# A planned attention and MLP kernel: its order learns when loads land, v's column bounds are taken later, and the first normalization is divided anew

## The chip, the cores and the metric

The kernel runs on one core of one Trainium2 chip. A core has five engines with a queue each, which run side by side and wait for one another through semaphores: TensorE (PE in the profile, its weight loads PEld), VectorE (DVE), ScalarE (ACT), GpSimd (POOL) and SyncE (SP), which here issues every DMA. Matrix products land in PSUM, eight banks of 2 KB in each of 128 partitions; everything else lives in SBUF. The metric is the device time of one execution in microseconds (us), the median over runs; lower is better.

## What is computed

One block: a layer norm modulated by a condition `c`, attention with 32 heads of width 16 over 2048 rows, a gated residual, then a second modulated norm, a mixer that shifts rows by one or two, and an MLP of width 1792. Cut to what matters here:

```python
mod = (silu(c) @ w_mod).reshape(1, 6, 1, -1)
sa, ca, ga, sb, cb, gb = (mod[:, i] for i in range(6))
h = layernorm(x) * (1 + ca) + sa
q, k, v = split_heads(h @ wqkv)                 # 32 heads, 16 wide
p = softmax(q @ k.T * 16 ** -0.5)
x = x + ga * (merge_heads(p @ v) @ wo)
h = layernorm(x) * (1 + cb) + sb
g = shift_rows(gelu(layernorm(h) @ w1))         # by +1, -1, +2, -2 in four quarters
x1 = h + g @ w2
x = x + gb * (x1 + gelu(layernorm(x1) @ w3) @ w4)
```

## The kernel before

**One order, written by a planner.** The program is not left to a scheduler: while it is built, the class `Sched` keeps a clock for each engine (`sch.T`, with "P" for TensorE and "S" for SyncE's DMA queue), a price for each operation, and decides what is issued next. The prices and the constants at the top of the file are only the planner's; the chip runs the order that comes out, each engine its own queue in sequence. So a constant that adds no instruction can move many.

**Ahead of attention.** The 2048 rows of x come in four chunks of 512 (`ci` 0 to 3). `ln1` takes statistics of four tiles of 128 rows on VectorE (L383, L384), their inverse deviation on GpSimd (L387, L388), and applies the norm tile by tile: on ScalarE (L562) for the tiles listed in `LNA[ci]`, else on VectorE (L559). `ln1_T` transposes on TensorE (L626) and modulates: for the columns in `LNV[ci]` ScalarE writes the high part (L635) and VectorE the whole (L638); else ScalarE does both (L631, L652). The low part of the split is taken on GpSimd for the columns in `LNG[ci]`, else on VectorE (both L644). `PST`, `PAP` and `PTR` rank these chains by chunk, lower first. Products of q, k and v in split precision (L372, L374, L376) follow; q, k and v are stored to DRAM.

**The bound of v.** `v_weights(a)` makes, for each half `a` of the heads, a bound of every column of v: TensorE sums (L825), `bound` clips (L831), then `cols` does three things on VectorE in one piece: two reductions against the identity, which bring the bound from a row into a column (`vcol`, L836), and the reciprocal of the row (L838). Then GpSimd scales the weights of v by that reciprocal (L844) and they are split (L471, L473). `vcol` is read when the pieces of the output projection are scaled (L914). The reductions write their unneeded product into one of the six `qk` buffers.

**Attention.** There are 64 units (4 chunks of queries by 16 pairs of heads) of 16 steps; a step is 128 keys, so there are 1024. Maxima run 24 steps (`LEAD`) ahead of scores: a row of work is one matmul for a maximum (mb, L1033) reduced on VectorE (L1029) beside one matmul of scores (sc, L1049) whose exponential ScalarE takes (L1045). When a unit's maxima are done, eight small DMAs write the shift rows into its q tile (qtl<-nm). Of each exponential the high half is used as it is, and the low half is made by GpSimd in one operation (L1104) or by ScalarE in two: `p_low`. Columns are the products with v (pv): high ones (L1130) for each step, low ones (L1127) for each two. Eight buffers (`NPT`) hold exponentials from the scores to the low columns.

**Who goes next.** The main loop turns between rows, columns and fillers. Fillers are everything else: the remaining q, k and v, the splitting of weights, and the whole block behind attention for earlier chunks (`tail`). `cols()` counts the columns that are ready by `col_at`, at most `CMOST`; rows may start when banks are free (`one`) and VectorE is about to run dry (`EARLY`); after rows, columns wait for fillers if the filler credit is over `OFIRST` and enough buffers are free. `DUES` is a curve: by that step so many us of filler should be done, from which the credit per step comes. `do_row` calls `p_low` for steps that lie `PLAG` behind.

**Loads.** `load_unit` brings a unit's q rows (three DMAs), zeros, and k rows (three DMAs); `load_v` brings v for four steps; all on SyncE's queue. `sch.dma` returns a modelled landing time, which these callers drop: the order assumes the data is there. On the chip the semaphores hold TensorE until it is.

Of the kernel before, what the change touches and what calls it, by code (L numbers as in the profile page):

```python
# [21 lines left out]
P = 128  # L22
# [15 lines left out]
DUES = ((20, 67.7), (60, 87.3), (85, 95.9), (122, 115.8), (150, 130.7), (205, 149.7), (245, 167.7),  # L38
        (505, 270.0), (765, 395.7), (1012, 527.8))
BTOP, BLOW = 1200.0, 300.0  # L40
LEAD = 24
LAG = 2
RES0 = 2
DMIN = 600.0
PAP = (1,0,-1,-1)
PST = (1,0,0,1)
PTR = (-1,1,1,0)
TRX = 140.0
DAP = 1000.0
# [35 lines left out]
LNA = ((1,2,3),(0,1,2,3),(3,),(3,))  # L85
LNG = ((0,1),(0,1,2,3),(0,2),(0,2))
LNV = ((),(),(1,2,3),(1,3))
# [12 lines left out]
PTLOW = 3  # L100
BACK = 100.0
EARLY = 200.0
OWE = 1500.0
PX = 265.0
# [239 lines left out]
def kernel(ctx, tc, A_x, A_wqkv, A_wo, B_w1, B_w2, B_w3, B_w4, c, w_mod, out):  # L344
# [272 lines left out]
    def ln1_T():  # L617
        for ci in range(NC):
            x = xt[ci]
            left = [KT]  # L620
            for k in range(KT):
# [31 lines left out]
                sch.chain(*ops, (e, 1320 if e == "G" else 670, low), (None, 0, one), prio=PTR[ci])  # L653
# [106 lines left out]
    direct, near = [], set()  # L760

    def v_tiles(w, a, kts):
        wh, wl = halves(w, KT)
        for kt in kts:
# [19 lines left out]
            def store(kt=kt, w=w):  # L784
                vrs[0] -= 1

                if not a and direct:
                    sch.dma(dma.dma_start, direct[kt // 4][:, kt % 4], w[:, 0])
                    near.add(kt)

                def gone():
                    vlive.remove(kt)
                    done.add(("vk", a, kt))
                    if kt % 4 == 3:
                        done.add(("v", a, kt // 4))
                e = sch.dma(dma.dma_start, Vs[8 * a:8 * a + 8, :, kt, :].rearrange("a p n -> p a n"),
                            w)
                sch.after(e, gone)
# [9 lines left out]
    def v_weights(a):  # L808
# [19 lines left out]
        scr = ab[0][:, :P]  # L828

        def bound():  # L830
            dve.tensor_scalar(vb, b, 1e-30, None, op0=OP.max)  # L831
            sch.free(b)

        def cols():
            for i in range(2):
                dve.tensor_tensor_reduce(out=scr, in0=vb[:, i * P:(i + 1) * P], in1=ident, scale=VHI, scalar=0.0,  # L836
                                         op0=OP.mult, op1=OP.add, accum_out=vcol[:, 2 * a + i:2 * a + i + 1])
            dve.reciprocal(vb, vb)  # L838
            qfree.extend(ts)

        def scaled():
            for i, (f, f3) in enumerate(st):
                c = slice(512 * i, 512 * i + 512)
                sch.chain(("G", 1500, lambda f3=f3: pool.tensor_tensor(f3, f3, vb[:, None, :].to_broadcast([P, 2, 256]),  # L844
                                                                       op=OP.mult)),
                          *split_chain(f, w[:, 0, c], w[:, 1, c], mark(keys[2 + i])), ready=sch.T["D"] + XX)
            done.add(("vcol", a))
        sch.chain(("D", cD(256), bound), ("D", 1900, cols), (None, 0, scaled), bank=b)
# [89 lines left out]
    def load_rows(t, src, pr, cs, to):  # L938
        for i in range(3):
            sch.dma(dma.dma_start, t[i + 1::4, to].bitcast(F32), src[2 * pr * DH:(2 * pr + 2) * DH, i, cs])  # L940
# [48 lines left out]
    def load_unit(u):  # L989
# [7 lines left out]
        load_rows(kst[u % 3], Ks, pr, slice(0, S), slice(0, S))  # L997
# [3 lines left out]
    def load_v(u, i):  # L1001

        if (u, i) in vnext or not u:
# [3 lines left out]
            sch.dma(dma.dma_start, vst[i], Vs[units[u][1], :, 4 * i:4 * i + 4])  # L1007
# [62 lines left out]
    def max_fin(u):  # L1070
# [4 lines left out]
        def shift_rows():  # L1075
            for j in range(2):
                for i in range(2):
                    r = 64 * j + 32 * i
                    for h in range(2):
                        sch.dma(dma.dma_start,  # L1080
# [520 lines left out]
    def before(s):  # L1601
# [12 lines left out]
        if s < VAT[0]:  # L1614
            for kt in range(4):
                if kt not in near and ("vk", 0, kt) in done:
                    near.add(kt)
                    sch.dma(dma.dma_start, vst[0][:, kt % 4], Vs[0, :, kt])
        if s in VAT:
            i = VAT.index(s)  # L1620
            for kt in range(4 * i, 4 * i + 4):
                while kt not in near and ("vk", 0, kt) not in done:
                    sch.step()
                if kt not in near:
                    sch.dma(dma.dma_start, vst[i][:, kt % 4], Vs[0, :, kt])
# [17 lines left out]
    def col_at(y):  # L1643
# [3 lines left out]
        return max(e_hi[s], v_free[0] if s % NKT == 0 else 0.0) if s in e_hi else LATE  # L1647
# [37 lines left out]
    while x < end or pvs or acs:  # L1685
# [14 lines left out]
        if can:  # L1700
# [4 lines left out]
            if one >= LATE:  # L1705
                one = free[need - 1]
            enter = (sch.mode != "r") * (SWITCH + ENTER)
# [87 lines left out]
```

## Time and profile before

| | us |
|---|---|
| median of 3 runs (1980.74 to 1981.08) | 1981.05 |
| the profiled execution | 1979.15 |
| its span, first to last instruction | 1977.4 |

The profile is of one execution. Busy times count an engine as busy while any of its instructions is under way; for TensorE that includes matmuls whose ends are modelled, so a full TensorE is not one at its peak. A window row gives busy time and number of instructions by engine, the granted clock of TensorE (1.00 is full), the busy share of the DMA engines, and GB/s. A row of waits names who waited for whom: us in total, times, longest. "issue" is waiting for nothing that the profile shows. Attention's exponentials run from 91.2 to about 1810 us; before that lies the preparation, after it the tail of the last chunk.

### The profile page before, as it was taken

The page shows a single profiled execution, that of the slowest core. Times are in us where ns is not written, and L with a number is a line of the kernel's source. Part 1 is how long each engine was busy: PE and PEld are TensorE (multiplying, and loading weights), DVE is VectorE, ACT ScalarE, POOL GpSimd, SP SyncE. Part 2 cuts the span into 40 slices and gives each one's busy share as a digit, 9 for nine tenths or more (in the row PEclk, how much of TensorE's full clock was granted, in tenths as well). Part 3 has the DMA queues.
Part 4 walks back from the last instruction along what each step waited for, and adds up shares of the span by engine and source line. Part 5 has one row for each costly group of instructions (what it writes and reads, how often), then busy time and mean ns, then how long its engine had stood idle before and what let it go on. Part 6 is the DMA issues. An engine that isn't in the chain of part 4 may idle for free.

```text
span 1977.4 us, 42253 instructions
## 1 busy us (share of the span) xinstructions
PE 1924.6 (97%) x14472; PEld 1126.1 (57%) x14472; DVE 1663.7 (84%) x3005; ACT 1490.4 (75%) x3106; POOL 1655.9 (84%) x1588
## 2 busy tenths in 40 slices
PE   7899999999999999999999999999999999999899
PEld 4655565455445555555446555555555555556798
DVE  7989888788999988888998989898998989882644
ACT  6476898678879787787988878787878777777443
POOL 6378999889999988898898999988899998996632
PEclk9999999999999999999999999999999999999999
DMA  5766777767632343434433233343433333333532
GB/s 205 209 186 213 219 225 251 227 215 256 205 113 88 112 152 112 140 110 143 132 111 116 88 113 119 116 138 129 154 115 94 111 113 116 116 117 130 195 136 91
DMA packets 233082, 293.23 MB, mean 148 GB/s; under 512 B 125876, under 2 KB 178052, under 8 KB 216580
## 3 DMA queue, kind: packets, MB, share of 16 engines
q1 hardware_dynamic: 232868, 290.53, 46.3%
q8 instruction: 115, 1.88, 0.4%
q14 instruction: 99, 0.81, 0.1%
HBM read 225.81 MB, written 62.91 MB: 146 GB/s over the span
## 4 chain that ended last, share of the span: by engine, by line
PE 73%; DVE 14%; ACT 4%; POOL 3%; DMA 3%; issue 2%; SPq 1%; POOLq 0%; ACTq 0%; DVEq 0%
PE mb L1033 15%; PE sc L1049 11%; PE pv L1130 10%; DVE mx L1029 8%; PE w L372 7%; PE w L376 7%; PE w L374 7%; PE pv L1127 6%; ACT pt L1045 2%; POOL pt L1104 1%; SPq L136 1%; PE ot L1162 1%; PE xT L1240 1%; DVE tst L383 1%; PE mr L674 1%
## 5 line engine op out<-in xcount | busy, mean ns | idle before, releaser
L1029 DVE TENSOR_REDUCE mx<-mb 128x1 f32<-128x512 f32 x2048 | 1284.5, 682 | 127.5 <-PE mb L1033 96.0
L1104 POOL TENSOR_SCALAR pt<-pt 128x1024 f16<-128x1024 uint16 x970 | 1289.8, 1367 | 88.2 <-ACT pt L1045 83.6
L1045 ACT ACTIVATE pt<-sc 128x512 int32<-128x512 f32 x2048 | 1097.3, 605 | 266.3 <-PE mb L1033 191.1
L1033 PE MATMUL mb<-kst,qtl 64*128 64x512 f32 x2048 | 753.9, 454 | 18.9 <-DVE mx L1029 6.4
L1049 PE MATMUL sc<-qtl,kst 64*128 64x512 f32 x2048 | 725.3, 444 | 1.2 <-ACT pt L1045 0.7
L1033 PEld LDWEIGHTS mb<-kst,qtl 64*128 64x128 f32 x2048 | 346.5, 192 | 231.0 <-DVE mx L1029 117.1
L1049 PEld LDWEIGHTS sc<-qtl,kst 64*128 64x128 f32 x2048 | 332.8, 185 | 153.0 <-issue 58.5
L1130 PE MATMUL pv<-pt,vst 128*32 128x512 f16 x4096 | 353.7, 393 | 1.7 <-DMA vst<-Vs 1.4
L1127 PE MATMUL pv<-pt,vst 128*17 128x512 f16 (+1 forms) x2048 | 214.4, 398 | 2.0 <-POOL pt L1104 2.0
L1130 PEld LDWEIGHTS <-vst 128*32 128x32 bf16 x4096 | 112.0, 95 | 112.8 <-issue 53.4
L1464 POOL TENSOR_TENSOR g<-xs,g 128x256 fp32r<-128x256 f32 (+2 forms) x144 | 103.0, 716 | 86.1 <-ACT g L1463 84.3
L372 PE MATMUL w<-A,wr 128*128 128x256 f32 (+2 forms) x576 | 172.2, 299 | 0.5 <-ACT A L366 0.3
L374 PE MATMUL w<-A,wr 128*128 128x256 f32 (+2 forms) x576 | 169.7, 295 | 0.5 <-DVE A L362 0.3
L376 PE MATMUL w<-A,wr 128*128 128x256 f32 (+2 forms) x576 | 170.0, 295 | 0.0
L1127 PEld LDWEIGHTS <-vst 128*25 128x25 f16 (+1 forms) x2048 | 55.5, 90 | 134.0 <-issue 117.6
L372 PE MATMUL w<-wr,g 128*128 128x512 f32 x288 | 118.6, 412 | 0.7 <-ACT g L1463 0.6
L372 PEld LDWEIGHTS w<-A,wr 128*128 128x128 f32 x576 | 109.9, 191 | 15.9 <-issue 8.8
L374 PE MATMUL w<-wr,g 128*128 128x512 f32 x288 | 117.6, 408 | 0.0
L376 PEld LDWEIGHTS w<-A,wr 128*128 128x128 f32 x576 | 109.7, 190 | 13.3 <-issue 13.3
L376 PE MATMUL w<-wr,g 128*128 128x512 f32 x288 | 117.1, 407 | 0.2 <-POOL g L1464 0.2
L374 PEld LDWEIGHTS w<-A,wr 128*128 128x128 f32 x576 | 109.8, 191 | 12.4 <-issue 10.9
L1460 ACT ACTIVATE sq<-w 128x256 f32<-128x256 f32 (+2 forms) x144 | 56.2, 391 | 56.4 <-PE w L376 55.2
(148 smaller groups left out, 2088.8 us busy)
## 6 DMA issues: line engine op xcount, KB each, us to landing
wr<-Ws SPq DMA_DIRECT2D x80, 1024.0 KB
kst<-Ks SPq DMA_DIRECT2D x189, 256.0 KB
vst<-Vs SPq DMA_DIRECT2D x252, 192.0 KB
qtl<-Qs SPq DMA_DIRECT2D x192, 64.0 KB
Vs<-vt SPq DMA_DIRECT2D x32, 384.0 KB
Ws<-wq SPq DMA_DIRECT2D x40, 256.0 KB
Ws<-wst SPq DMA_DIRECT2D x40, 256.0 KB
wst<-in_B_w_dram SPq DMA_DIRECT2D x36, 256.0 KB
```

The costliest lines, as they stand in the source:

```text
L372: te.matmul(o, lh, rh, start=first, stop=False)
L374: te.matmul(o, lh, rl, start=False, stop=False)
L376: te.matmul(o, ll, rh, start=False, stop=last)
L1029: end = sch.crit("D", 605, e + PX, lambda: dve.reduce_max(mxs[u][:, j, g, c:c + 1], b, axis=AX.X))
L1033: return ready, lambda: te.matmul(b, lhs, kst[u % 3][r, c * CH:(c + 1) * CH], start=True, stop=True), after
L1045: ea = sch.crit("A", 480, e + PX, lambda: act.activation(pt[s][:, j], b, AF.Exp))
L1049: return ready, lambda: te.matmul(b, kst[u % 3][r, kt * P:(kt + 1) * P], qst[u][r], start=True, stop=True), after
L1104: e_low[s] = XP["G"] + sch.crit("G", 1345, ready, lambda: pool.tensor_scalar(o, i, 0.5, 1.0, op0=OP.mult, op1=OP.mult))
L1127: te.matmul(acc[r:r + n, :], v[:, (kt + i) % 4, c - n:c].bitcast(F16), pt[s + i].bitcast(F16)[:, j, 0::2], start=False, stop=kt == NKT - 2 ...
L1130: te.matmul(acc[r:r + 32, :], v[:, kt % 4, r:r + 32], pt[s].bitcast(F16)[:, j, 1::2], start=kt == 0, stop=False, skip_group_check=True)
L1460: sch.chain(("A", cA(n), lambda: act.activation(sq, b, AF.Square, scale=2.0)), ("D", cD(n), cube), ("A", cA(n), lambda: act.activation(sq, ...
L1464: ("G", cG(n), lambda: pool.tensor_tensor(lo, xs, hi, op=OP.subtract)), (None, 0, end), bank=b)
```

## The change

It does six things.

- Loads return their modelled landing, kept in `came`: by unit for q and k rows, by unit and quarter for v, and under "s" for shift rows. `one`, the earliest start of a row, now is no earlier than the landing of the q and k rows of the maxima's unit and of the shift rows of the scores' unit; a high column is ready no earlier than the landing of its v.
- In `v_weights`, `bound` is followed by the reciprocal alone. The two reductions come in a chain of their own, on the reciprocal, ready 30 us later (`VCAT`) and of rank 3, into a tile of their own; a reciprocal of 128 x 2 brings the bound back. The chain of the bound has rank 0 (`PVB`).
- `LNA`, `LNG` and `LNV` divide the first normalization otherwise; `PAP`, `PST` and `PTR` rank it otherwise; the planner's price of an application on VectorE (`DAP`) and of the low part on VectorE is higher.
- `DUES` asks for about 4 us more filler up to step 765 and 7.8 us less by step 1012.
- `EARLY` is 300 for 200, `OFIRST` 1000 for 1500, `CMOST` 7 for 6, `PLAG` 2 for 1.
- `XX` is 165 for 170.

```diff
-DUES = ((20, 67.7), (60, 87.3), (85, 95.9), (122, 115.8), (150, 130.7), (205, 149.7), (245, 167.7),
-        (505, 270.0), (765, 395.7), (1012, 527.8))
+DUES = ((20, 71.8), (60, 91.4), (85, 100), (122, 121), (148, 135.5), (205, 153.8), (245, 171.8),
+        (505, 274.1), (765, 399.8), (1012, 520))
+PVB = 0
+VCAT = 30000.0
-PAP = (1,0,-1,-1)
-PST = (1,0,0,1)
-PTR = (-1,1,1,0)
+PAP = (-1, 0, 1, -1)
+PST = (-1, 0, 0, 1)
+PTR = (2, -1, 0, -1)
-DAP = 1000.0
+DAP = 1300.0
-LNA = ((1,2,3),(0,1,2,3),(3,),(3,))
-LNG = ((0,1),(0,1,2,3),(0,2),(0,2))
-LNV = ((),(),(1,2,3),(1,3))
+LNA = ((1, 2, 3), (0, 1, 2, 3), (1, 2, 3), (1, 2, 3))
+LNG = ((0, 1), (0, 1, 2), (0, 1, 2, 3), (0,))
+LNV = ((1,), (1,), (0, 1, 3), (3,))
+XX = 165.0
+PX = 265.0
-EARLY = 200.0
-OWE = 1500.0
-PX = 265.0
+EARLY = 300.0
+OFIRST = 1000.0
+CMOST = 7
+PLAG = 2
...
-                sch.chain(*ops, (e, 1320 if e == "G" else 670, low), (None, 0, one), prio=PTR[ci])
+                sch.chain(*ops, (e, 1320 if e == "G" else 900, low), (None, 0, one), prio=PTR[ci])
...
-        scr = ab[0][:, :P]
+        scr = qp.tile([P, P], F32, name="scr", tag="scr", bufs=1)
+        v2 = vcol[:, 2 * a:2 * a + 2]
 
         def bound():
             dve.tensor_scalar(vb, b, 1e-30, None, op0=OP.max)
             sch.free(b)
-
-        def cols():
-            for i in range(2):
-                dve.tensor_tensor_reduce(out=scr, in0=vb[:, i * P:(i + 1) * P], in1=ident, scale=VHI, scalar=0.0,
-                                         op0=OP.mult, op1=OP.add, accum_out=vcol[:, 2 * a + i:2 * a + i + 1])
-            dve.reciprocal(vb, vb)
             qfree.extend(ts)
+
+        def cols(i):
+            dve.tensor_tensor_reduce(out=scr, in0=vb[:, i * P:(i + 1) * P], in1=ident, scale=1.0 / VHI, scalar=0.0,
+                                     op0=OP.mult, op1=OP.add, accum_out=v2[:, i:i + 1])
+            if i:
+                dve.reciprocal(v2, v2)
...
-            done.add(("vcol", a))
-        sch.chain(("D", cD(256), bound), ("D", 1900, cols), (None, 0, scaled), bank=b)
+            sch.chain(("D", 450, partial(cols, 0)), ("D", 600, partial(cols, 1)), mark(("vcol", a)), prio=3, ready=sch.T["D"] + VCAT)
+        sch.chain(("D", cD(256), bound), ("D", 1700, lambda: dve.reciprocal(vb, vb)), (None, 0, scaled), prio=PVB, bank=b)
...
-            sch.dma(dma.dma_start, t[i + 1::4, to].bitcast(F32), src[2 * pr * DH:(2 * pr + 2) * DH, i, cs])
+            e = sch.dma(dma.dma_start, t[i + 1::4, to].bitcast(F32), src[2 * pr * DH:(2 * pr + 2) * DH, i, cs])
+        return e
...
-        load_rows(kst[u % 3], Ks, pr, slice(0, S), slice(0, S))
+        came[u] = load_rows(kst[u % 3], Ks, pr, slice(0, S), slice(0, S))
...
-            sch.dma(dma.dma_start, vst[i], Vs[units[u][1], :, 4 * i:4 * i + 4])
+            came[u, i] = sch.dma(dma.dma_start, vst[i], Vs[units[u][1], :, 4 * i:4 * i + 4])
...
-        return max(e_hi[s], v_free[0] if s % NKT == 0 else 0.0) if s in e_hi else LATE
+        return max(e_hi[s], v_free[0] if s % NKT == 0 else 0.0, came.get((s // NKT, s % NKT // 4), 0.0)) if s in e_hi else LATE
...
             if one >= LATE:
                 one = free[need - 1]
+            one = max(one, came.get((s + LEAD) // NKT, 0.0), came.get(("s", s // NKT), 0.0))
```

More of the change, by code (lines that the diff above doesn't have):

```diff
@@ L759 @@
     vlive, vrs = [], [0]
-    direct, near = [], set()
+    direct, near, came = [], set(), {}
     def v_tiles(w, a, kts):
@@ L787, in store @@
                 if not a and direct:
-                    sch.dma(dma.dma_start, direct[kt // 4][:, kt % 4], w[:, 0])
+                    came[0, kt // 4] = sch.dma(dma.dma_start, direct[kt // 4][:, kt % 4], w[:, 0])
                     near.add(kt)
@@ L1079, in shift_rows @@
                     for h in range(2):
-                        sch.dma(dma.dma_start,
+                        came["s", u] = sch.dma(dma.dma_start,
                                 qst[u][r:r + 1, h * 256:(h + 1) * 256].bitcast(F32).rearrange("o (p l) -> o p l", l=2),
@@ L1617, in before @@
                     near.add(kt)
-                    sch.dma(dma.dma_start, vst[0][:, kt % 4], Vs[0, :, kt])
+                    came[0, 0] = sch.dma(dma.dma_start, vst[0][:, kt % 4], Vs[0, :, kt])
         if s in VAT:
@@ L1624, in before @@
                 if kt not in near:
-                    sch.dma(dma.dma_start, vst[i][:, kt % 4], Vs[0, :, kt])
+                    came[0, i] = sch.dma(dma.dma_start, vst[i][:, kt % 4], Vs[0, :, kt])
         if s == NS - 12:
```

## The prediction

> **What bounds the kernel now.** I read the page first: the busy times and the chain of waits.
>
> ```profile
> span 1977.4 us, 42253 instructions
> PE 1924.6 (97%) x14472; PEld 1126.1 (57%) x14472; DVE 1663.7 (84%) x3005; ACT 1490.4 (75%) x3106; POOL 1655.9 (84%) x1588
> PE 73%; DVE 14%; ACT 4%; POOL 3%; DMA 3%; issue 2%; SPq 1%; POOLq 0%; ACTq 0%; DVEq 0%
> ```
>
> TensorE has work 97% of the span, so only 1977.4 - 1924.6 = 52.8 us are free of any matmul; a change that leaves the matmuls as they are can win idle time, a lowered clock, or turns between kinds of matmul. The waits of the weight loads, longest first, show the turns:
>
> ```profile
> PEld L1127 <- issue: 117.6, 374, 2.3
> PEld mb L1033 <- DVE mx L1029: 117.1, 311, 1.0
> PEld sc L1049 <- issue: 58.5, 166, 0.6
> PEld L1130 <- issue: 53.4, 186, 0.5
> ```
>
> The three rows "issue" are turns at which nothing is waited for: 117.6 + 58.5 + 53.4 = 229.5 us in 726 turns, 0.32 us each. Every planner constant acts through their number. Next the windows, by stage: where do TensorE, VectorE and the clock stand?
>
> ```profile
> core 0: us, PE busy (x) PEld busy (x) DVE busy (x) ACT busy (x) POOL busy (x), PEclk, DMA share, GB/s
> 32.70:38.00 5.30, 5.30 (x35) 4.49 (x34) 5.27 (x7) 5.27 (x10) 4.63 (x4) 1.00 0.55 206
> 38.00:46.00 8.00, 5.10 (x29) 3.70 (x28) 7.86 (x10) 4.67 (x9) 5.95 (x6) 1.00 0.34 110
> 46.00:54.50 8.50, 6.42 (x34) 4.89 (x34) 7.61 (x10) 4.49 (x9) 2.73 (x2) 1.00 0.49 184
> 59.00:80.00 21.00, 18.34 (x108) 12.81 (x105) 20.57 (x38) 6.59 (x17) 7.21 (x8) 1.00 0.89 226
> 110.00:120.00 10.00, 10.00 (x74) 7.14 (x72) 3.07 (x6) 4.30 (x11) 3.46 (x4) 1.00 0.79 241
> 380.00:400.00 20.00, 15.68 (x90) 8.04 (x89) 8.96 (x16) 8.88 (x19) 13.52 (x13) 0.74 0.47 150
> ```
>
> Three things are to be seen. From 32.70 to 54.50 VectorE works 5.27 + 7.86 + 7.61 = 20.74 of 21.80 us while TensorE works 16.82: the stage ahead of attention goes at VectorE's pace. So does the first filling of maxima (20.57 of 21.00). And at 380 to 400 TensorE, VectorE and ScalarE all sag and the granted clock is 0.74: a stall. From 600 us on no wait for a DMA stands among TensorE's own; the longest is the first row of that answer:
>
> ```profile
> PE mb L1033 <- DVE mx L1029: 4.3, 14, 0.5
> ```
>
> **The change, part by part.** *First normalization divided anew, and v's bound.* The instructions on VectorE's path, from the timeline and from the lines' own rows:
>
> ```profile
> 29.79 0.97 DVE L559 TENSOR_SCALAR xt<-xt,mv,rs 128x512 f32<-128x512 f32 x2
> 32.70 4.34 DVE L559 TENSOR_SCALAR xt<-xt,mv,rs 128x512 f32<-128x512 f32 x4
> 38.00 0.34 DVE L836 CUSTOM_DVE_ANT_0 qk<-vb,ident 128x128 f32<-128x128 f32 x1
> 38.39 1.27 DVE L836 CUSTOM_DVE_ANT_0 qk<-vb,ident 128x128 f32<-128x128 f32 x1
> 39.70 1.75 DVE L838 RECIPROCAL vb<-vb 128x256 f32<-128x256 f32 x1
> L559 DVE TENSOR_SCALAR xt<-xt,mv,rs x7: 512/543/1507, 14.7 to 35.5; 128x512 f32<-128x512 f32 x7
> L562 ACT ACTIVATE xt<-xt,rs x9: 797/801/817, 14.9 to 34.3; 128x512 f32<-128x512 f32 x9
> L638 DVE TENSOR_SCALAR h<-tr,modcol x5: 712/798/802, 41.4 to 50.8; 128x512 f32<-128x512 f32 x5
> L652 ACT ACTIVATE hT<-h x11: 629/632/642, 19.4 to 47.8; 128x512 fp32r<-128x512 f32 x11
> ```
>
> LNA sends tiles 1 and 2 of chunks 2 and 3 to ScalarE. The two L559 at 29.79 and the four at 32.70 are these two chunks' tiles 0 to 2 in order, so one of the first two (0.97/2 = 0.49) and three of the four (3 x 4.34/4 = 3.26) go: 3.7 us off VectorE (2.0 at the shortest duration, 0.512 each). The two reductions of L836 leave the place between bound and reciprocal: 39.70 - 38.00 = 1.7 us, and GpSimd's scaling, which waits for the reciprocal, starts as much earlier. LNV has six entries instead of five: one more L638 (+0.8) and one L652 less on ScalarE (-0.6). LNG still has ten. VectorE's net is -3.7 - 1.7 + 0.8 = -4.6; ScalarE's is 4 x 0.80 - 0.63 = +2.6. ScalarE is full from 32.70 to 38.00 (5.27 of 5.30) but has 16.5 - 9.16 = 7.3 us left of the next 16.5. Between 4.6 (all of it shows) and 4.6 - 2.6 = 2.0 (ScalarE's load delays the transposes fully) I take 3.0. The ends: 6 us gained if TensorE's 38.00-to-54.50 gaps (16.5 - 11.5 = 5.0) and a little of the entry go too; 2.6 lost if the path turns out to be ScalarE's.
>
> The L836 pair comes back some 30 us later (VCAT) on VectorE's queue, in front of maxima if no gap is found, because VectorE is full until the first exponentials at 91 us. It took 0.34 and 1.27 here; I charge 0.5, since 110 to 120 has 7 us of VectorE free; if that cover is missed, 2.5 (2 x 1.27). The second half (a=1) does the same near 174 us and hides. Who reads the columns is far away:
>
> ```profile
> L914 ACT ACTIVATE wst<-wst,vcol x4: 706/714/762, 322.4 to 348.9; 128x512 f32<-128x512 f32 x4
> ```
>
> At one such place a page speaks against the move. The Trainium skill, "SBUF — State Buffer", section "Who interferes with whom", says that a VectorE instruction with two SBUF inputs blocks against a GpSimd instruction that reads SBUF. The spread of L836 (0.34 and 1.27, the second beside GpSimd's work) agrees; by that rule alone both later reductions would cost 1.27 and the sum of this part would be 2.0 us worse.
>
> **First part: -3.0 + 0.5 = -2.5 us.** No DMA moves with it; two of the six qk buffers return before the reciprocal instead of after it.
>
> *Landings known to the order.* The stall, from the timeline:
>
> ```profile
> 382.78 0.40 PE L1127 MATMUL pv<-pt,vst 128*25 128x512 f16 x3 [1.74 <-POOL pt L1104]
> 382.80 1.76 SPq L136 DMA_DIRECT2D qtl<-Qs  x3
> 385.26 1.75 SPq L136 DMA_DIRECT2D kst<-Ks  x3
> 390.88 0.76 PE L1033 MATMUL mb<-kst,qtl 64*128 64x512 f32 x1 [2.58 <-DMA vst<-Vs]
> 549.32 0.63 PE L1130 MATMUL pv<-pt,vst 128*32 128x512 f16 x8 [1.42 <-DMA vst<-Vs]
> ```
>
> The q and k rows of a new unit were issued from 382.80 to 387.01, and the unit's first maximum stood at TensorE's head until 390.88 (the row names v, but its operands are kst and qtl). With `came` the planner puts that row behind columns and fillers until the modelled landing. No semaphore or instruction is added: what is queued behind such a row is the reduction on VectorE and the exponential on ScalarE that each row feeds, and the columns that need those. The 1.74 us for GpSimd before it is not touched. Idle at 380 to 400 is 20 - 15.68 = 4.32 us; a clock of 0.74 during 15.68 busy us costs about 0.26 x 15.68 = 4.1 more; 8.4 is the upper end. Of it the row's wait (2.58) and about half of the clock's loss (2.0) belong to the landing: I take 4.5; lower end 0, where nothing is there to fill. The v wait at 549.32 is the other kind (columns, `came[u, i]`): 1.4 at most, 1.0 taken.
>
> The clock's share is where a rule and the trace part. The Trainium skill, "TensorE: Matmul & The Clock Gate", Part 1, has the clock halved only after an idle window of about 3.4 us; here the longest idle time of TensorE in the stretch is 2.58 us and the granted clock is nonetheless 0.74, so the trace doesn't agree with the plain reading. By the page alone, the wait would give back 2.6 and not 4.5, and the sum would be 1.9 smaller.
>
> **Second part: -4.5 - 1.0 = -5.5 us.** After 600 us there is no DMA wait to win, and the same additions can only shuffle the order.
>
> *Constants.* XX, DAP, the cost of `low` and PVB alter the planner's figures or ranks alone. DUES asks for 4.1 us more filler early (67.7 to 71.8), the same slope after it, and 7.8 less by step 1012. TensorE is full either way, as two windows near the end show:
>
> ```profile
> 1780.00:1790.00 10.00, 10.00 (x85) 5.53 (x84) 1.50 (x4) 10.00 (x24) 10.00 (x10) 1.00 0.44 136
> 1830.00:1840.00 10.00, 6.35 (x27) 4.82 (x27) 9.21 (x22) 1.63 (x2) 4.57 (x10) 0.89 0.82 280
> ```
>
> Filler moved within full stretches costs nothing; moved into the gap at 1830 it could win 3.6; if it is short where VectorE alone is full it loses as much. EARLY, OFIRST, CMOST and PLAG shift when rows, columns and fillers take turns. Nothing here shows their sign: 0, with 2% of the 229.5 us of turns to either side, 4.6. GpSimd's halving (L1104) hides PLAG's later place as long as buffers of exponentials are free.
>
> **Sum:** -2.5 - 5.5 + 0 = -8.0 us. The profiled execution took 1979.15 us (1.75 of it outside the span), so the changed kernel would take 1971.15 there; the median of the runs is 1981.05, 1.9 above it, so I forecast 1981.05 - 8.0 = 1973.0.
>
> **The rivals.** *A. The landing is known but the hole stays.* If at the new unit neither columns nor filler with credit stand ready, the planner only lets time pass, and TensorE waits as before. For it: at 380 to 400 VectorE and ScalarE starve with TensorE, so few columns were ready. Against: q matmuls were in hand at 384.6 and 395.0. Only the first part is left: 1981.05 - 2.5 = 1978.5.
>
> *B. Fewer turns.* If CMOST 7 and OFIRST 1000 lengthen the groups by 2%, 4.6 us come on top: 1973.0 - 4.6 = 1968.4. For it: 726 turns at 0.32; against: EARLY 300 lets rows in sooner, which makes turns.
>
> *C. Low halves come late (slower).* PLAG 2 puts GpSimd's or ScalarE's halving of a step one step later in the queues, behind other work. Each step holds one of eight buffers from its scores until the low columns. The chain by line, a wait, and the first and last exponentials:
>
> ```profile
> PE mb L1033 15%; PE sc L1049 11%; PE pv L1130 10%; DVE mx L1029 8%; PE w L372 7%; PE w L376 7%; PE w L374 7%; PE pv L1127 6%; ACT pt L1045 2%; POOL pt L1104 1%; SPq L136 1%; PE ot L1162 1%; PE xT L1240 1%; DVE tst L383 1%; PE mr L674 1%
> POOL pt L1104 <- ACT pt L1045: 83.6, 137, 4.4
> ...
> L1045 ACT ACTIVATE pt<-sc x9: 578/597/611, 91.2 to 99.5; 128x512 int32<-128x512 f32 x9
> ...
> L1045 ACT ACTIVATE pt<-sc x143: 577/598/662, 1701.3 to 1809.6; 128x512 int32<-128x512 f32 x143
> ```
>
> GpSimd's halving is 1% of the chain, about 20 us, though GpSimd sits idle 83.6 us waiting for exponentials: it now starts as soon as they come. With exponentials from 91 to 1810 us over 1024 steps a step is 1.68 us; each step that finds no buffer free costs up to that. Five such steps (8.4) cancel the forecast; from eight on it is slower than the bound below. If the 20 us rise by three quarters, 15 are lost: 1973.0 + 15 = 1988.0. Against: GpSimd's other work is what PLAG lets pass, and it feeds fillers.
>
> **How the numbers follow.** Forecast 0.48, A 0.20, B 0.14, C 0.18. A measurement of this kernel tells about 0.2% from no change, 4.0 us: below 1977.1 is faster, above 1985.0 slower. Forecast and B are faster, 0.62; A is same, 0.20; C is slower, 0.18. The range for 8 in 10 runs from 1961.0 (6.0 + 8.4 + 1.4 + 4.6 = 20.4 gained) to 1988.0 (C's middle); the forecast's own is 1967 to 1977.
>
> **What would show it.** The first maximum stands here:
>
> ```profile
> L1033 PE MATMUL mb<-kst,qtl x59: 386/499/508, 58.3 to 99.4; 64*128 64x512 f32 x59
> ```
>
> Right: L559 three times and L562 thirteen, the first maximum some 3 us ahead of 58.3; no drop of the clock near 390; no wait for kst or vst over 1 us on TensorE; the rows of turns within 2%. Wrong: ScalarE in place of VectorE on the chain before 55 us; a hole of the same length at a new unit (A); GpSimd's pt above 1% of the chain and fewer maxima per 200 us between 600 and 1800 (C). What I can't see from here is the order that the planner lays out: a small edit moves every later choice, and its sum may exceed every term above.

## The result, and the profile after

The changed kernel takes **1966.60 us** (median of 4 runs, 1966.41 to 1966.67) beside 1981.07 us of the kernel before on the same chip (4 runs, 1980.74 to 1984.37): a ratio of 0.9926, 95% interval 0.9913 to 0.9939, so 14.5 us less. The forecast was 1973.0, 8.0 less. The profiled execution took 1966.6 us with a span of 1964.8, 12.6 shorter than the span before.

The page of the kernel after, its span, busy times and chain:

```profile
span 1964.8 us, 42299 instructions
PE 1913.2 (97%) x14472; PEld 1120.9 (57%) x14472; DVE 1658.0 (84%) x3004; ACT 1491.0 (76%) x3103; POOL 1654.6 (84%) x1591
PE 57%; DVE 8%; ACT 3%; POOL 2%; issue 1%; DMA 1%; SPq 0%; POOLq 0%; ACTq 0%; DVEq 0%
```

The matmuls are the same 14472, and TensorE is again busy 97% of the span: on these lines alone nothing happened. Free of any matmul are 1964.8 - 1913.2 = 51.6 us, 1.2 less than before. The gain lies inside "busy", where a matmul that ends late and one that runs at pace look alike. So the windows come next (columns as in the table of before: busy time and instructions of TensorE, its weight loads, VectorE, ScalarE and GpSimd, then the granted clock):

```profile
core 0: us, PE busy (x) PEld busy (x) DVE busy (x) ACT busy (x) POOL busy (x), PEclk, DMA share, GB/s
38.00:46.00 8.00, 8.00 (x46) 6.73 (x45) 6.90 (x8) 7.86 (x13) 6.37 (x6) 1.00 0.56 204
46.00:54.50 8.50, 7.37 (x48) 6.08 (x46) 5.88 (x9) 4.51 (x12) 2.82 (x3) 1.00 0.69 228
300.00:450.00 150.00, 147.55 (x1101) 76.70 (x1093) 132.97 (x221) 123.22 (x245) 143.89 (x120) 1.00 0.75 238
380.00:400.00 20.00, 20.00 (x149) 10.59 (x141) 18.28 (x32) 15.81 (x32) 19.30 (x17) 1.00 0.54 180
```

TensorE's gaps before attention are smaller (8.00 busy for 5.10, 7.37 for 6.42), and the hole at 380 to 400 is gone: 149 matmuls where 90 stood, at full clock. Over 300 to 450 the kernel before did 1029 matmuls where this one does 1101:

```profile
300.00:450.00 150.00, 143.93 (x1029) 76.12 (x1026) 121.93 (x203) 116.22 (x233) 131.15 (x110) 0.97 0.73 234
```

The entry, after: rows of the normalization, the maxima and the exponentials of the first 100 us.

```profile
L564 DVE TENSOR_SCALAR xt<-xt,mv,rs x3: 526/539/1162, 15.4 to 38.4; 128x512 f32<-128x512 f32 x3
L567 ACT ACTIVATE xt<-xt,rs x13: 797/802/815, 14.9 to 37.6; 128x512 f32<-128x512 f32 x13
L1040 PE MATMUL mb<-kst,qtl x61: 385/499/507, 55.5 to 99.5; 64*128 64x512 f32 x61
L1052 ACT ACTIVATE pt<-sc x20: 579/597/607, 88.6 to 106.5; 128x512 int32<-128x512 f32 x20
```

VectorE applies three tiles and ScalarE thirteen; the first maximum is at 55.5 (58.3 before) and the first exponential at 88.6 (91.2): 2.6 to 2.8 us. The last exponential, before and then after, is only 3.4 us earlier:

```profile
L1045 ACT ACTIVATE pt<-sc x24: 592/614/651, 1794.7 to 1809.6; 128x512 int32<-128x512 f32 x24
```

```profile
L1052 ACT ACTIVATE pt<-sc x16: 594/641/765, 1796.7 to 1806.2; 128x512 int32<-128x512 f32 x16
```

From there to the end it is 1977.4 - 1809.6 = 167.8 us before and 1964.8 - 1806.2 = 158.6 after: **9.2 of the 12.6 us are won behind the last exponential**, where the forecast took nothing: it named the gap at 1830 to 1840 us, at 3.6 at most, and left it out of its sum. The groups of TensorE from the last exponential to the end, before and then after (name and shape, times | busy us, mean ns), show what is missing there:

```profile
L372 PE MATMUL w<-wr,g 128*128 128x512 f32 x98 | 38.8, 396 | 0.6 <-ACT g L1463 0.6
L372 PE MATMUL w<-A,wr 128*128 128x256 f32 x104 | 30.4, 293 | 0.3 <-ACT A L366 0.3
L1240 PE MATMUL xT<-ident,osb 128*128 128x128 f32 x16 | 2.2, 272 | 0.0
```

```profile
L377 PE MATMUL w<-wr,g 128*128 128x512 f32 x92 | 36.3, 395 | 1.4 <-ACT g L1470 1.4
L377 PE MATMUL w<-A,wr 128*128 128x256 f32 x88 | 25.7, 292 | 0.3 <-ACT A L371 0.3
L1247 PE MATMUL xT<-ident,osb 128*128 128x128 f32 x4 | 0.7, 286 | 0.0
```

Sixteen transposes of the last chunk's output (osb) waited until the exponentials were done; now twelve of them, and 16 of 104 products of one kind in each of three split parts (L372, L374 and L376 before; one of the three is shown), are filler during attention. In attention itself TensorE did that work and still finished earlier.

The waits of the weight loads after, which answer to the four rows shown of before:

```profile
PEld L1134 <- issue: 123.2, 396, 1.0
PEld mb L1040 <- DVE mx L1036: 104.5, 268, 1.0
PEld sc L1056 <- ACT pt L1052: 59.9, 155, 0.7
PEld sc L1056 <- issue: 40.5, 113, 0.5
...
PEld L1137 <- issue: 21.2, 73, 0.4
```

Turns cost 123.2 + 40.5 + 21.2 = 184.9 us in 582, for 229.5 in 726. But scores wait for ScalarE 59.9 us in 155 where it was:

```profile
PEld sc L1049 <- ACT pt L1045: 34.3, 94, 0.7
```

So the order has 144 turns fewer, 44.6 us of them, and part comes back as another wait at the same place.

### The profile page after: what moved, and what is told of

It reads as the page before. It is cut to its first block, busy times and chain, and to the rows that moved or that the text cites. A ratio compares the mean times of both kernels' runs of the same rounds, so it can differ in the third digit from the quotient of the medians.

```text
span 1964.8 us, 42299 instructions
## 1 busy us (share of the span) xinstructions
PE 1913.2 (97%) x14472; PEld 1120.9 (57%) x14472; DVE 1658.0 (84%) x3004; ACT 1491.0 (76%) x3103; POOL 1654.6 (84%) x1591
## 4 chain that ended last, share of the span: by engine, by line
PE 57%; DVE 8%; ACT 3%; POOL 2%; issue 1%; DMA 1%; SPq 0%; POOLq 0%; ACTq 0%; DVEq 0%
PE mb L1040 12%; PE sc L1056 9%; PE pv L1137 8%; PE w L377 7%; PE w L379 7%; PE w L381 7%; DVE mx L1036 5%; PE pv L1134 5%; ACT pt L1052 2%; POOL pt L1111 1%; PE ot L1169 1%; PE xT L1247 1%; DVE tst L388 1%; PE wo L381 1%; DMA out_dram<-x 1%
## 5 line engine op out<-in xcount | busy, mean ns | idle before, releaser
L1111 POOL TENSOR_SCALAR pt<-pt 128x1024 f16<-128x1024 uint16 x973 | 1287.0, 1369 | 21.1 <-ACT pt L1052 19.8
L1056 PEld LDWEIGHTS sc<-qtl,kst 64*128 64x128 f32 x2048 | 333.4, 184 | 165.9 <-ACT pt L1052 59.9
L1137 PE MATMUL pv<-pt,vst 128*32 128x512 f16 x4096 | 335.3, 391 | 0.6 <-DMA vst<-Vs 0.6
L1137 PEld LDWEIGHTS <-vst 128*32 128x32 bf16 x4096 | 108.8, 95 | 87.1 <-issue 21.2
L1134 PEld LDWEIGHTS <-vst 128*25 128x25 f16 (+1 forms) x2048 | 55.2, 90 | 139.0 <-issue 123.2
```

Of the source, the lines that this page charges most:

```text
L1056: return ready, lambda: te.matmul(b, kst[u % 3][r, kt * P:(kt + 1) * P], qst[u][r], start=True, stop=True), after
L1111: e_low[s] = XP["G"] + sch.crit("G", 1345, ready, lambda: pool.tensor_scalar(o, i, 0.5, 1.0, op0=OP.mult, op1=OP.mult))
L1134: te.matmul(acc[r:r + n, :], v[:, (kt + i) % 4, c - n:c].bitcast(F16), pt[s + i].bitcast(F16)[:, j, 0::2], start=False, stop=kt == NKT - 2 ...
L1137: te.matmul(acc[r:r + 32, :], v[:, kt % 4, r:r + 32], pt[s].bitcast(F16)[:, j, 1::2], start=kt == 0, stop=False, skip_group_check=True)
```

## The experiments

The theory to test was the prediction's own: the hole near 390 goes because the order knows the landings, the entry is worth 2 to 3 us, and the constants nothing. The rivals: the constants do it, through turns; or no edit does it, and the two kernels are two draws from a planner whose order any edit shuffles. Twelve kernels were run, in three groups with runs of the kernel before beside each (its medians 1982.97, 1980.82 and 1981.67; single runs 1978.96 to 1985.74). "Profile" times below are of one execution of each. Losses are counted from the 1966.60 above; the kernel before moved by 2.2 us between the groups, so 2 us or less tell nothing.

### One part of the change undone at a time

**No landings.** The order ignores `came` in both places; it is the same as the changed kernel's up to about step 248.

```diff
-        return max(e_hi[s], v_free[0] if s % NKT == 0 else 0.0, came.get((s // NKT, s % NKT // 4), 0.0)) if s in e_hi else LATE
+        return max(e_hi[s], v_free[0] if s % NKT == 0 else 0.0) if s in e_hi else LATE
...
-            one = max(one, came.get((s + LEAD) // NKT, 0.0), came.get(("s", s // NKT), 0.0))
```

> The changed kernel with the two uses of the landing times taken out (rows and high columns no longer wait for them in the plan); all else as changed. Local theory (the prediction's terms add up): the landings are worth 5.5, so 1966.6 + 5.5 = 1972.1 us, with a sunken clock and a wait of TensorE for k rows near 390 us back. Turns theory (the gain beyond the front comes from fewer turns between rows, columns and fillers, which the constants make): within 2 us of 1966.6, no matter whether the stall returns or not, and TensorE's idle turns stay as after. Scatter theory (every edit of the plan moves all later choices by some us either way): anything from 1960 to 1973, with no stall needed to explain it.

Measured: 1966.03 us (1964.66 to 1967.10), 0.9920 of before [0.9905, 0.9935]. Its window:

```profile
380.00:400.00 20.00, 20.00 (x151) 10.48 (x149) 18.35 (x31) 16.30 (x33) 19.31 (x17) 1.00 0.53 167
```

No hole, without any knowledge of landings. In the traces of these two kernels the queues of VectorE, ScalarE, GpSimd and the DMAs hold the same operations in the same order until after 500 us, so at 380 to 400 the landings had not altered the order at all. In this kernel that part is worth nothing that can be measured (-0.6 us), and my reason for the largest term falls. The landings alone were not added to the kernel before; what they would do to its hole is not shown.

**Old constants.**

```diff
-EARLY = 300.0
-OFIRST = 1000.0
-CMOST = 7
-PLAG = 2
+EARLY = 200.0
+OFIRST = 1500.0
+CMOST = 6
+PLAG = 1
```

> The changed kernel with EARLY, OFIRST, CMOST and PLAG as before (200, 1500, 6, 1). Local theory: these are worth nothing, 1966.6 us within 2. Turns theory: the gain beyond the front and the stall goes, 14.5 - 8.0 = 6.5 us slower, 1973 us, and TensorE's idle turns before high columns (21.2 us in 73 after, 53.4 in 186 before) come back. Scatter theory: 1960 to 1973 without the turns telling which.

Measured: 1977.66 us (1974.52 to 1980.82, 10 runs), 0.9974 [0.9964, 0.9984]: 11.1 of the 14.5 us are lost. Its last exponential stands at 1801.3, *ahead* of the changed kernel's 1806.2, but the span ends at 1975.6, 174.3 later. Its groups from there to the end, and its waits:

```profile
L1247 PE MATMUL xT<-ident,osb 128*128 128x128 f32 x16 | 2.2, 272 | 0.0
```

```profile
PEld L1134 <- issue: 114.3, 371, 0.9
...
PEld sc L1056 <- issue: 58.0, 174, 0.5
PEld L1137 <- issue: 52.2, 180, 0.6
...
PEld sc L1056 <- ACT pt L1052: 33.4, 93, 0.6
```

All sixteen transposes are behind the end again, and the turns are back at 224.5 us in 725. Both signs belong to the constants, then. The turns theory had them return too, but at 6.5 us.

**Old front**: the first normalization's division, ranks and prices, and the place and rank of v's bound, as before (the rest of the change stays).

```diff
-PAP = (-1, 0, 1, -1)
+PAP = (1,0,-1,-1)
...
-LNA = ((1, 2, 3), (0, 1, 2, 3), (1, 2, 3), (1, 2, 3))
+LNA = ((1,2,3),(0,1,2,3),(3,),(3,))
...
-        def cols(i):
+        def cols():
+            for i in range(2):
...
-        sch.chain(("D", cD(256), bound), ("D", 1700, lambda: dve.reciprocal(vb, vb)), (None, 0, scaled), prio=PVB, bank=b)
+        sch.chain(("D", cD(256), bound), ("D", 1900, cols), (None, 0, scaled), bank=b)
```

> The changed kernel with the first normalization divided and ranked as before and v's column bounds taken in their old place. Local theory: the first maximum goes from 55.5 back to 58.3 us and the whole loses that, 1966.6 + 2.8 = 1969.4 us. Turns theory: the same 2.8. Scatter theory: the front loses 2.8 at the first maximum, but the end may lie 5 us to either side of it, 1964 to 1974.

Measured: 1988.99 us (1986.04 to 1990.96, 5 runs), 1.0039 [1.0025, 1.0054]. 22.4 us lost by undoing what I had priced at 2.5; none of the theories above allowed for that. Its two halves were then undone alone. (What they expect of a catch-up theory is set out under DAP 1310 below.)

**Old place and rank of v's bound.**

```diff
...
-            sch.chain(("D", 450, partial(cols, 0)), ("D", 600, partial(cols, 1)), mark(("vcol", a)), prio=3, ready=sch.T["D"] + VCAT)
-        sch.chain(("D", cD(256), bound), ("D", 1700, lambda: dve.reciprocal(vb, vb)), (None, 0, scaled), prio=PVB, bank=b)
+            done.add(("vcol", a))
+        sch.chain(("D", cD(256), bound), ("D", 1900, cols), (None, 0, scaled), bank=b)
```

> The changed kernel with v's column bounds taken in their old place and the old rank of that chain; the first normalization as changed. Local theory: the two reductions and the rank are worth 1.7 us, 1968.3. Catch-up theory: unit 12's loads come three steps late in the planner's order, steps 128 to 192 take 117 us or more, the whole 1975 to 1985 us, though the first maximum moves by less than 2 us.

Measured: 1974.63 us (1972.81 to 1975.52, 6 runs), 0.9964 [0.9951, 0.9978]: 8.0 lost.

**Old normalization**: `PAP`, `PST`, `PTR`, `DAP`, `LNA`, `LNG`, `LNV` and the price of the low part as before.

```diff
...
-DAP = 1300.0
+DAP = 1000.0
...
-LNA = ((1, 2, 3), (0, 1, 2, 3), (1, 2, 3), (1, 2, 3))
+LNA = ((1,2,3),(0,1,2,3),(3,),(3,))
...
```

> The changed kernel with the first normalization divided, ranked and priced as before; v's column bounds as changed. Local theory: VectorE gets four applications back, 1.3 to 3 us, 1968 to 1970. Catch-up theory: no unit is late in the planner's order, steps 128 to 192 take 107 to 111 us, and the whole is 1967 to 1972 us; a result of 1975 or more with that stretch short would speak against it.

Measured: 1972.08 us (1968.43 to 1979.53, 8 runs), 0.9953 [0.9941, 0.9964]: 5.5 lost. Two halves that cost 8.0 and 5.5 alone cost 22.4 together, and neither half alone starts well: the first exponential is at 93.6 with v's bound old and at 95.7 with the normalization old, *later* than with both old (92.0).

**Old curve of dues.**

```diff
-DUES = ((20, 71.8), (60, 91.4), (85, 100), (122, 121), (148, 135.5), (205, 153.8), (245, 171.8),
-        (505, 274.1), (765, 399.8), (1012, 520))
+DUES = ((20, 67.7), (60, 87.3), (85, 95.9), (122, 115.8), (150, 130.7), (205, 149.7), (245, 167.7),
+        (505, 270.0), (765, 395.7), (1012, 527.8))
```

> The changed kernel with the old curve of due times. Local theory: no cost, since TensorE is full wherever filler is moved, 1966.6 us within 2. Turns theory: the same. Rival: the later part of the curve (520 in place of 527.8 by step 1012) is what lets filler fall into the tail's gap, whose first 30 us of TensorE idle 6 us before: then 3 to 5 us slower, 1970 to 1972, with the tail longer by as much.

Measured: 1973.91 us (1970.64 to 1978.62, 6 runs), 0.9962 [0.9947, 0.9977]: 7.3 lost. The rival had 3 to 5 by a longer tail, but from the last exponential to the end it takes 157.5 us, no longer than the 158.6 of the changed kernel: the loss lies earlier. The undone parts sum to -0.6 + 11.1 + 22.4 + 7.3 = 40.2 us, almost three times the whole gain of 14.5. Such numbers can't be shares of it.

### Edits with no content

So the next kernels change a price in the planner by so little that it says nothing about the chip, as a measure of what shuffling alone does. Three start from the changed kernel:

```diff
-DAP = 1300.0
+DAP = 1310.0
```

> The changed kernel with one planner price moved by 10 ns: DAP 1310 for 1300. It adds and removes nothing. Local theory: 1966.6 us within 2. Catch-up theory (the gain by step 512 is that the fillers which units 8 and 12 need, the second half of v and the third group of k and q, are done in time, so that the planner need not stop rows to force them): the planner's order then has unit 12's loads four steps late, as before the change, and steps 128 to 192 take 117 to 125 us on the chip in place of 107.5 after (121.1 before, 125.6 with the old front); the whole 1974 to 1981 us. Scatter theory without a place: some us to either side, not in that stretch.

```diff
-XX = 165.0
+XX = 170.0
```

> The changed kernel with XX 170 as before in place of 165: a planner's allowance between engines, 5 ns. Local theory: 1966.6 us within 2. Catch-up theory: no unit is late, steps 128 to 192 take 107 to 111 us; the rest scatters, 1962 to 1972 us. It shows how far the order alone moves the time when no unit is late.

```diff
-VCAT = 30000.0
+VCAT = 31000.0
```

> The changed kernel with VCAT 31000 in place of 30000, so that the two column reductions are ready 1 us later in the plan; nothing added or removed. Local theory: 1966.6 us within 2. Scatter theory: 1961 to 1976 us. Selected-order theory: 1972 to 1981 us, never below 1966.

Measured: 1980.79 us (ratio 1.0005 [0.9993, 1.0016]), 1976.59 (0.9978 [0.9967, 0.9989]) and 1968.09 (0.9935 [0.9912, 0.9959]): **14.2 and 10.0 us slower for 10 ns and 5 ns in one planner's price**, and 1.5 for 1 us, which is not clear of the noise (single runs 1964.41 to 1975.77). The first gives back the whole gain. The local theory, 1966.6 within 2, is out by the first two; the third lies below the 1972 of the selected-order theory and within the scatter theory's 1961 to 1976.

The catch-up theory is out as well. By the starts of the exponentials (two to a step), steps 128 to 192 took 110.5 us with DAP 1310, where it asked for 117 to 125; 115.2 with XX 170, for 107 to 111; 113.4 with v's bound old, for 117 or more; and 121.7 with the normalization old, for 107 to 111. Two start from the kernel before; one of them takes nothing but the change's own `XX`:

```diff
+XX = 165.0
```

> The kernel before with XX 165 in place of 170, a part of the change by itself and 5 ns in a planner's allowance. Local theory: 1981 us within 2. Scatter theory (any edit of the planner's numbers draws another order out of a spread of some 5 us to either side): 1976 to 1986 us. Selected-order theory (before and after are each a lucky order among their neighbours, since such edits of the changed kernel cost 10 and 14 us): 1986 to 1996 us, and then the changed kernel's neighbourhood is the better one by as much as its own centre shows (about 1977 to 1981).

```diff
+PLOAD = 3600.0
```

> The kernel before with the planner's pause between two weight pieces at 3600 in place of 3500 ns; nothing added or removed. Local theory: 1981 us within 2. Scatter theory: 1976 to 1986 us. Selected-order theory: 1986 to 1996 us.

Measured: 1998.08 us (ratio 1.0078 [1.0061, 1.0095]) and 1989.9 (1.0044 [1.0027, 1.0060]; one execution of 5469.7 us is left out): 16 and 8 us slower than the 1981.67 beside them, both more than the scatter theory's 5. By these two neighbours and those three, the kernel before is a good draw among its own, and the changed one among its own.

### The constants alone on the kernel before

```diff
+EARLY = 300.0
+OFIRST = 1000.0
+CMOST = 7
+PLAG = 2
```

> The kernel before with EARLY 300, OFIRST 1000, CMOST 7 and PLAG 2 alone. Turns theory: TensorE's idle turns before high columns fall from 53.4 us in 186 to about 25 in 85, and the time by the 11 us that undoing them cost the changed kernel: 1970 us. Scatter theory: the turns fall alike, but the waits for ScalarE and VectorE take their place, and the time lies anywhere from 1975 to 1990 us.

Measured: 1987.38 us (1982.62 to 1993.43, 10 runs), 1.0028 [1.0016, 1.0040], 5.7 slower and not the 1970 of the turns theory. By times alone the constants cost 5.7 here and win 11.1 there. By the profile both agree: its waits, and its transposes from the last exponential to the end, are

```profile
PEld sc L1053 <- ACT pt L1049: 51.7, 138, 0.9
...
PEld sc L1053 <- issue: 39.6, 108, 0.5
```

```profile
L1244 PE MATMUL xT<-ident,osb 128*128 128x128 f32 x4 | 0.7, 286 | 0.0
```

Fewer turns to scores (39.6 us for 58.5), more waits of scores for ScalarE, four transposes for sixteen: the constants' marks. What is lost lies earlier, with a last exponential at 1822.1, beside 1825.1 and 1817.1 of the two neighbours of before.

### All kernels side by side

A single time says little here, but fourteen profiles do. "Q's store": the start of the first store of q rows after 318 us; "steps ahead": by how many steps the loads of unit 12 run ahead of its own first step, counted from the exponentials (a unit loaded in time runs about 32.5 ahead, and its maxima are due 24 ahead); "matmuls": TensorE's instructions in the window 300 to 450 and its granted clock; "wait": the longest single wait of TensorE in that window; "behind": span less last exponential. All but the last column are of the one profiled execution, which can lie off the median: 7.5 us above it with the old normalization, 3.5 below it with the constants added to the kernel before.

| kernel | normalization | v's bound | constants | q's store | steps ahead | matmuls, clock | wait | last exponential | behind | median us |
|---|---|---|---|---|---|---|---|---|---|---|
| before | old | old | old | 375.1 | 26.5 | 1029, 0.97 | 2.6 | 1809.6 | 167.8 | 1981.1 |
| before, XX 165 | old | old | old | 387.4 | 27.5 | 1008, 0.95 | 3.3 | 1825.1 | 171.5 | 1998.1 |
| before, PLOAD 3600 | old | old | old | 380.5 | 26.5 | 1019, 0.97 | 4.3 | 1817.1 | 173.6 | 1989.9 |
| before, new constants | old | old | new | 379.6 | 29.5 | 1026, 0.98 | 6.5 | 1822.1 | 160.0 | 1987.4 |
| after, old front | old | old | new | 383.7 | 28.5 | 1033, 0.98 | 5.3 | 1826.6 | 157.7 | 1989.0 |
| after, old normalization | old | new | new | 362.8 | 32.5 | 1027, 0.98 | 4.1 | 1820.3 | 157.5 | 1972.1 |
| after, old v's bound | new | old | new | 368.4 | 30 | 1111, 1.00 | 0.4 | 1812.4 | 158.6 | 1974.6 |
| after, old constants | new | new | old | 368.7 | 28.5 | 1078, 1.00 | 1.4 | 1801.3 | 174.3 | 1977.7 |
| after, DAP 1310 | new | new | new | 376.2 | 28 | 1113, 1.00 | 0.6 | 1820.3 | 158.6 | 1980.8 |
| after, XX 170 | new | new | new | 350.9 | 32.5 | 1069, 1.00 | 1.4 | 1815.6 | 158.8 | 1976.6 |
| after, old dues | new | new | new | 354.3 | 32.5 | 1098, 1.00 | 1.2 | 1816.7 | 157.5 | 1973.9 |
| after, VCAT 31000 | new | new | new | 351.9 | 32.5 | 1072, 1.00 | 0.3 | 1806.7 | 159.8 | 1968.1 |
| after, no landings | new | new | new | 350.9 | 32.5 | 1094, 1.00 | 0.6 | 1805.3 | 157.6 | 1966.0 |
| after | new | new | new | 352.1 | 32.5 | 1101, 1.00 | 0.6 | 1806.2 | 158.6 | 1966.6 |

Three marks split the kernels cleanly.

- **Behind the last exponential** it is 167.8 to 174.3 us in all four kernels with the old constants and 157.5 to 160.0 in all ten with the new. That is 7.8 us at least, through every shuffle. Sixteen transposes of osb lie behind in those four, four in these ten. But part of the work is paid for earlier: on average the last exponential comes 7.1 us later with the new constants and the old front (two kernels beside three), and 10.5 later with the new front (six beside one). Which of the four constants does it wasn't tried.
- **In 300 to 450** all six kernels with the old normalization do 1008 to 1033 matmuls at a clock under 1.00, all eight with the new one 1069 to 1113 at 1.00. The means are 1023.7 and 1092; at the pace of the faster ones the difference is 150 x (1 - 1023.7/1092) = 9.4 us, an estimate that takes all matmuls as alike. Steps 128 to 192, which lie in this window, split the same way: 121.1 to 133.5 us in the six, 106.9 to 115.2 in the eight. So does the longest wait, 2.6 us or more in the six and 1.4 or less in the eight.
- **q's store and unit 12.** Where the store comes at 368.4 or later, unit 12 is loaded 26.5 to 30 steps ahead instead of 32.5, without exception. The later the store, the longer the kernel, with few exceptions (rank correlation 0.89 over the fourteen).

The long waits of the six have three causes. Those of the five that are not the kernel before, in the order of the table:

```profile
PE mb L1034 <- DMA kst<-Ks: 3.3, 1, 3.3
PE mb L1034 <- DMA kst<-Ks: 4.3, 1, 4.3
PE mb L1037 <- DVE qk L366: 6.5, 1, 6.5
PE pv L1133 <- POOL pt L1110: 6.0, 2, 5.3
PE sc L1056 <- DVE qk L367: 4.1, 1, 4.1
```

The first two are the hole of the kernel before: TensorE waits for the rows of unit 12. In the third and fifth it waits for an operation of VectorE that stands behind a held one (last section). In the fourth it waits for low halves, before which GpSimd scales weights (331.86 to 335.53 us).

The late unit is where the hole of before comes from. The timeline of before, in the prediction, had the loads of q at 382.80. In the kernel after, and in the one with the old constants, they are:

```profile
371.00 1.77 SPq L141 DMA_DIRECT2D qtl<-Qs  x3
```

```profile
374.30 1.76 SPq L141 DMA_DIRECT2D qtl<-Qs  x3
```

They can't go before that unit's q rows are stored, and that store (before, then after, first of the two times) is the thing that moved by 23 us:

```profile
L136 SPq DMA_DIRECT2D Qs<-qk x2: 319/344/370, 375.1 to 375.8; - x2
```

```profile
L141 SPq DMA_DIRECT2D Qs<-qk x4: 379/412/520, 352.1 to 376.9; - x4
```

The maximum at TensorE's head at 390.88 waited for rows that were *issued* late, because the filler that makes them came late. How late is too late can be worked out: at 26.5 steps ahead only 2.5 steps are left until the maxima, 4.2 us at 1.68 us a step, and issuing the unit's rows alone took that long (382.80 to 387.01). The three kernels with 26.5 or 27.5 steps have the hole; those with 28 or more wait 1.4 us for these rows at most. Where the rows come in time, knowing when they land adds nothing. Whether it helps where they are late is open: the three with the hole don't know the landings, and of the five at 28 to 30 steps all but one do.

How the first normalization, over by 55 us, leads to a tighter order at 300 to 450 isn't settled: no resource links the two, only the planner's order, and the six lose their time there in the three ways shown. The one with only the normalization old may belong to them by its profiled execution alone, which is 7.5 us above its median.

Averages over the groups, by medians: old front and old constants 1989.7 (three kernels), old front and new constants 1988.2 (two), new front and old constants 1977.7 (one), new front and new constants 1972.0 (six). So the front is worth some 12 to 16 us and the constants 1.5 to 6, with 15 us between the best and worst of the last group: sizes with few samples. No kernel is clearly better than the changed one; the one without landings equals it.

## Why the prediction was right, and where it was not

The direction and the range were right, the size was not (14.5 for 8.0), and the parts were right by luck more than by reason.

- **First part, -2.5.** At its own place right to 0.1: first exponential 91.2 to 88.6. The shift was read rightly too: from 32.70 to 54.50 VectorE works 15.51 us for 20.74 (forecast -4.6) and ScalarE 17.41 for 14.43 (+2.6), and ScalarE did not become the bound, though it is nearly full from 38 to 46 (7.86 of 8.00): TensorE is 8.00 busy there. The reductions that come back later took 0.28 to 1.35 us each, about what they took before (0.34 and 1.27):

```profile
L842 DVE CUSTOM_DVE_ANT_0 scr<-vb,ident x4: 279/282/1347, 70.3 to 213.5; 128x128 f32<-128x128 f32 x4
```

  The first two came at 70.30 and 72.04 us between maxima, not in the free stretch at 110 to 120 that the charge of 0.5 rested on, and cost little because they took 0.28 each. The rival price, 1.27 for both, did not come: GpSimd was idle at the first and only filling kst from 72.10 at the second. The one of 1.35 (213.53 to 214.88) lies beside a GpSimd operation from 213.43 to 214.80. But in the kernel before the one of 0.34 lay beside GpSimd's work too (35.28 to 39.51), so such a neighbour alone doesn't decide.

  As a term of the sum the first part was mis-sized: undoing it costs 22.4, and the old normalization goes with some 9 us in 300 to 450. That its halves add up was luck: with either half alone the first exponential comes later than with neither.
- **Second part, -5.5: this step failed.** "Of it the row's wait (2.58) and about half of the clock's loss (2.0) belong to the landing" is wrong for the changed kernel; without landings the hole is just as absent. The hole's place and size were read rightly and its going was forecast, but I took the wait's last link (a DMA that landed late) for the cause and didn't ask why it had been issued late. The late unit could be read from the profile of before: the q store at 375.1, then the loads at 382.80.
- **Constants, 0 within 4.6: mis-sized.** "The rows of turns within 2%" was wrong by a factor of ten: 726 turns became 582. The price of 0.32 us a turn did not hold either as a gain: waits for ScalarE at the scores rose by 25.6 us. What counted was filler moved from behind the last exponential to before it. I saw the gap at 1830 to 1840, priced it at 3.6 us at most and took 0; the stretch behind the last exponential became 9.2 shorter. That isn't all gain, since with the new constants the last exponential tends to come later (table), but in this pair it did not.
- **Rivals.** A (the hole stays) is out. C (low halves late) is out: GpSimd's halving is still 1% of the chain (of the others, the one with the old front has a wait of 5.3 us for late low halves). What changed is that it no longer waits for exponentials, 19.8 us for 83.6 (67.9 with the old constants, 23.5 with the constants alone on the kernel before):

```profile
L1111 POOL TENSOR_SCALAR pt<-pt 128x1024 f16<-128x1024 uint16 x973 | 1287.0, 1369 | 21.1 <-ACT pt L1052 19.8
```

  B (fewer turns) had the right sign, at a tenth of the number.
- **The last sentence** ("a small edit moves every later choice, and its sum may exceed every term above") proved the strongest statement: 10 ns in a price moved the time by 14.2 us.

So the change is a gain as a whole (of the six kernels with front and constants new, five lie 4 us or more below all three with both old, and the sixth, DAP 1310, equals the kernel before). But its 14.5 us are also the distance between two well chosen orders, and can't be split into shares by undoing one part at a time.

## What to carry to other kernels

Where an order is fixed at build time by a planner, run a few neighbours with meaningless edits before a gain is credited to an edit; here their scatter, up to 16 us, is as large as the gain. Then compare marks in the profile that hold through the shuffles (work left behind the last exponential, matmuls in a stretch), not times. And follow a late DMA back to why it was issued when it was, before crediting whatever waits for it better.

## What the runs showed of the hardware

A VectorE instruction with two inputs in SBUF can be held for as long as GpSimd goes on without a gap. The timelines of the kernel with the old normalization, GpSimd first and then VectorE (start, duration, instruction):

```profile
324.35 1.28 POOL L935 TENSOR_TENSOR wst<-wst,wq 128x512 fp32r<-128x512 f32 x1
325.59 1.29 POOL L922 TENSOR_TENSOR wst<-wst,sbrow 128x512 f32<-128x512 f32 x1
326.86 3.85 POOL L1111 TENSOR_SCALAR pt<-pt 128x1024 f16<-128x1024 uint16 x3
...
324.47 6.73 DVE L476 TENSOR_TENSOR wp<-wst,wp 128x512 fp32r<-128x512 f32 x1 [0.45 <-POOL pt L1111]
331.13 0.68 DVE L367 TENSOR_TENSOR qk<-k,qk 128x512 fp32r<-128x512 f32 x1
```

The operation's median in that kernel is 0.92 us (14 of them); this one took 6.73, from just behind GpSimd's first instruction to 0.5 us past the end of its fifth (326.86 + 3.85 = 330.71). The windows show the others beside it: TensorE is short of 4.2 us in 20, and the clock falls.

```profile
320.00:330.00 10.00, 7.74 (x47) 4.17 (x45) 8.93 (x7) 7.42 (x15) 10.00 (x9) 1.00 0.73 213
330.00:340.00 10.00, 8.04 (x36) 3.50 (x36) 7.74 (x12) 3.37 (x6) 2.07 (x2) 0.66 0.82 300
```

The same stands in the kernel before with new constants:

```profile
336.94 1.36 POOL L920 TENSOR_TENSOR wst<-wst,sbrow 128x512 f32<-128x512 f32 x1
338.21 3.92 POOL L1108 TENSOR_SCALAR pt<-pt 128x1024 f16<-128x1024 uint16 x3
342.00 1.32 POOL L933 TENSOR_TENSOR wst<-wst,wq 128x512 fp32r<-128x512 f32 x1
343.23 1.39 POOL L1108 TENSOR_SCALAR pt<-pt 128x1024 f16<-128x1024 uint16 x1
...
337.01 8.09 DVE L475 TENSOR_TENSOR wp<-wst,wp 128x512 fp32r<-128x512 f32 x1
```

It ends at 345.10, 0.5 us past GpSimd's 344.62. Of the fourteen profiles four hold one such instruction (4.9 to 8.1 us), the kernels before and after none, and each ends 0.5 us past the end of GpSimd's stretch without a gap.

Such holds are the exception. In the fourteen traces 197 operations of the two kinds wp<-wst,wp and wst<-wst,wq began while GpSimd had more than 2 us of work without a gap (over 0.1 us) before it; 193 of them took 0.68 to 2.35 us. Those that began while GpSimd was idle took 0.69 at most. What sets the four apart is not known. The Trainium skill, "SBUF — State Buffer", section "Who interferes with whom", has a VectorE instruction with two inputs in SBUF contend with a GpSimd instruction that reads SBUF, and the issue order decide who blocks. The traces agree on the pair, and GpSimd had issued first in the two holds shown; but these held over several of GpSimd's instructions, five of them in the first. Whether such holds come in every execution of an order wasn't measured; the profiled execution of the kernel with the old normalization, 1979.53 us, is 7.5 above its median.
